# Output matmuls after a per-step plan with a queue, and a last block whose outputs keep tokens on partitions

## The chip, the core and the metric

The kernel runs on one core of a Trainium2 chip. The metric is the device time in microseconds (us), the median over several runs. Engines that matter: PE (TensorE matmuls), DVE (VectorE), ACT (ScalarE), POOL (GpSimd), and the queues that issue DMAs: SP's, ACT's and POOL's.

## The reference

Four batches of 12416 tokens with 128 channels. Per batch, 32 inducing vectors first attend over all tokens, then the tokens attend over the 32 results; a gated layer with 1536 hidden columns follows.

```python
def mab(q, kv):
    s = scale * (q @ kv.transpose(0, 2, 1))
    s = s - s.max(-1, keepdims=True)
    a = np.exp(s)
    a /= a.sum(-1, keepdims=True) + 1e-09
    return a @ kv
h = mab(I, x)
x = mab(x, h).astype(np.float32)
gate = 1.0 / (1.0 + np.exp(-(x @ w_gate)))
val = x @ w_val
out = (gate * val @ w_out).astype(np.float32)
```

The kernel never forms the second attention's output. It multiplies `h` into the weights first (`hw = h @ w_gate` and `h @ w_val`, 32 rows for each batch), so a token's gate and value columns are its 32 attention weights times `hw`. The sigmoid is computed as a tanh: with T = tanh(g/2), gate times value is 0.5 (T + 1) v.

## The kernel before

**Blocks and steps.** Tokens are taken in 97 blocks: 24 per batch of 512 tokens each, and one mixed last block of 4 times 128 tail tokens. The 1536 hidden columns are 12 chunks `j` of 128. The main loop (L709) does a block `n` in four steps `k`; step `k` handles the chunks 3k, 3k+1 (called va) and 3k+2 (vb). All engines follow the order of the program (`manual_schedule`, L70), each in its own queue.

In a step PE first fills the PSUM tile `va` (two matmuls, `v_fill`), then one pair of gate chunks `g` (`g_next`, `g_fill`), then some output matmuls, then `vb`, then in k1 and k3 a second `g` pair, or in k2 of some blocks a side job, and then more output matmuls. ACT turns each `g` pair into T (`g_tanh`, L421). DVE computes u = (T + 1) v, once for `va` and once for `vb` (`v_mul`, L434). The output matmuls (`out_mm`, L450) add `w_out` times u into one accumulator tile per block; after the twelfth, `out_store` (L455) scales it by 0.5 on ACT into `oT` (L460), transposes it by a DMA from SP (L462), and POOL stores it (L465, for the last block L472).

**Which output matmuls stand where.** They always belong to the u of the step before (`prev`, three of them). The first `first` of them go ahead of `vb`, the rest after it:

```python
first = 0 if k == 1 else 1
outs(prev[:first])
```

So a block's twelve outputs start in its k1 and end in k0 of the next block, after that step's `vb`.

**Tiles.** PSUM: `g` has two slots, shared with side jobs; `va`, `vb` and the accumulator `acc` have one each (L60 to L63). The gate pairs lead by three (`LEADP`). Most `g` and all `va` matmuls contract over 32 rows and take a quarter of the array each, so four of them run side by side; two of the six gate pairs (2 and 5) and all `vb` use weights padded with zeros to all 128 rows (`hwp`, `PADG`, `PADV`), the full array.

**Side jobs** (`put`, `extra`, `do_extra`, L650): work for the next batch and for later blocks, in k2 of 15 blocks of 24 for the first three batches and of three in the last, besides one in block 0 (batch-relative: s2 in 2, 10, 18; s1 in 4, 8, 11; s1t in 5; h in 7, 9, 12 to 15; hfin in 16; hw in 17). s1 and s2 end in an exp on ACT, h in an addition into `hacc` on DVE. Loads of x (`load_x`, POOL), transposes (`xT_dma`, SP) and the attention weights of later blocks are attached to steps by `at`.

**Start.** The six quarters of 2048 tokens of batch 0 are loaded by POOL, each with one DMA, then the weights. For each quarter, PE transposes 16 chunks (`xT_pe`; the first half is copied by ACT, the second by DVE), computes scores (`s1n`, with an exp on ACT) and adds them into h (`h_mm`).

Of the kernel before, what the change touches and what calls it, by code (L numbers as in the profile page):

```python
# [1 line left out]

# [6 lines left out]
F32 = mybir.dt.float32  # L9
F16 = mybir.dt.float16  # L10
AF = mybir.ActivationFunctionType
# [4 lines left out]
P = 128  # L16
TOK = 512
QT = 4 * TOK
M = 32
# [3 lines left out]
def kernel(  # L23
# [9 lines left out]
    nc = tc.nc  # L33
    B, N, C = x.shape
    m = inducing.shape[0]
    F = moe_w_gate.shape[1]
    NJ = F // P
    NP2 = NJ // 2
    SCALE = float(1.0 / (C ** 0.5))
    NQ = N // QT  # L40
    TAIL = N - NQ * QT
    NT0 = NQ * QT
# [5 lines left out]
    const = ctx.enter_context(tc.tile_pool(name="const", bufs=1))  # L48
    pers = ctx.enter_context(tc.tile_pool(name="pers", bufs=1))
    xtp = ctx.enter_context(tc.tile_pool(name="xtp", bufs=2))  # L50
    xqp = ctx.enter_context(tc.tile_pool(name="xqp", bufs=7))
    ep = ctx.enter_context(tc.tile_pool(name="ep", bufs=2))
    ap_ = ctx.enter_context(tc.tile_pool(name="ap", bufs=2))
    repp = ctx.enter_context(tc.tile_pool(name="repp", bufs=2))
    tp = ctx.enter_context(tc.tile_pool(name="tp", bufs=2))
    up = ctx.enter_context(tc.tile_pool(name="up", bufs=6))
    outp = ctx.enter_context(tc.tile_pool(name="outp", bufs=3))
    smp = ctx.enter_context(tc.tile_pool(name="smp", bufs=2))

# [5 lines left out]
    def slot_g(name):  # L65
        return ps_g.tile([P, 2 * TOK], F32, tag="g", name=name)
# [7 lines left out]
    def slot_o(name):  # L74
        return ps_o.tile([P, TOK], F32, tag="acc", name=name)
# [4 lines left out]
    xqs = {}  # L80

    def load_x(b, q):
        t = xqp.tile([P, QT], F16, tag="xq", name=f"xq_{b}_{q}")
        nc.gpsimd.dma_start(  # L84
            t[:], x[b, ds(q * QT, QT)].rearrange("(p j) c -> p (j c)", j=QT // P)
        )
        xqs[(b, q)] = t
# [4 lines left out]
    def load_tail(b):  # L92
# [12 lines left out]
    wo16 = const.tile([P, NJ, C], F16, tag="wo16")  # L105
    ident = const.tile([P, P], F16, tag="ident")
# [5 lines left out]
        out=ident[:], in_=ident[:], compare_op=ALU.not_equal, fill=1.0, base=0,  # L112
        pattern=[[-1, P]], channel_multiplier=1,
    )
    for q in range(2, NQ):
        load_x(0, q)
    nc.gpsimd.dma_start(wg16[:], moe_w_gate.rearrange("c (j f) -> c j f", f=P))
    nc.gpsimd.dma_start(wv16[:], moe_w_val.rearrange("c (j f) -> c j f", f=P))
    nc.gpsimd.dma_start(wo16[:], moe_w_out.rearrange("(j p) c -> p j c", p=P))
    nc.gpsimd.memset(stack[:], 0.0)  # L120
    for r in range(4):
        nc.gpsimd.affine_select(
            out=stack[:], in_=stack[:], compare_op=ALU.not_equal, fill=1.0,
# [3 lines left out]
    xTs = [xtp.tile([P, NT0], F16, tag="xT", name=f"xT_{b}") for b in range(B)]  # L127
# [23 lines left out]
    a1n = {}  # L151
# [23 lines left out]
    def s1n_mm(ps, b, q, lo, hi):  # L175
        for tk in range(lo, hi):
            j, r = tk % 4, tk // 4
            nc.tensor.matmul(
                ps[:, ds((j * 4 + r) * M, M)], xTs[b][:, ds(q * QT + tk * P, P)], indT[:],
                start=True, stop=True,  # L180
            )
# [10 lines left out]
    def h_mm(ps, b, q, first, last, tail, ch=0, cs=P):  # L192
        for j in range(4):
            nc.tensor.matmul(  # L194
                ps[:, cs:cs + P], ones[:, 0:P], a1n[(b, q)][:, j, :],
                start=first and j == 0, stop=last and j == 3,
            )
            if tail and j == 0:
                nc.tensor.matmul(
                    ps[:, cs:cs + M], ones[:, 0:P], a1n[(b, "t")][:], start=False, stop=False  # L200
                )
        for j in range(4):
            for r in range(4):
                nc.tensor.matmul(  # L204
                    ps[r * M:(r + 1) * M, ch:ch + P],
                    a1_chunk(b, q, 4 * r + j),
                    xqs[(b, q)][:, ts(4 * r + j, P)],
                    start=first and j == 0,
                    stop=last and j == 3 and not (tail and r == 0),
                )  # L210
        if tail:
            nc.tensor.matmul(
                ps[0:M, ch:ch + P], a1n[(b, "t")][:], xtail[:, b, :], start=False, stop=last,
            )
# [133 lines left out]
    NBK = len(blocks)  # L348
# [60 lines left out]
    Ts = {}  # L409
# [20 lines left out]

    def v_mul(ps, bi, j0, n):
        T = blocks[bi]["T"]
        u = up.tile([P, 2, TOK], F16, tag="u", name=f"u_{bi}_{j0}")
        nc.vector.scalar_tensor_tensor(  # L434
            out=u[:, 0:n, 0:T], in0=Ts[bi][:, j0:j0 + n, 0:T], scalar=1.0,
            in1=ps[:].rearrange("p (a t) -> p a t", t=TOK)[:, 0:n, 0:T],
            op0=ALU.add, op1=ALU.mult,
        )
        return [(bi, j0 + jj, u[:, jj, 0:T]) for jj in range(n)]

    accs = {}
    done_out = {}

    def out_mm(bi, j, u):
        T = blocks[bi]["T"]
        if bi not in accs:
            accs[bi] = slot_o(f"acc_{bi}")
            done_out[bi] = 0
        c = done_out[bi]
        nc.tensor.matmul(  # L450
            accs[bi][:, 0:T], wo16[:, j, :], u, start=(c == 0), stop=(c == NJ - 1)
        )
        done_out[bi] = c + 1

    def out_store(bi):  # L455
        k = blocks[bi]
        T = k["T"]
        nch = T // P
        oT = outp.tile([P, TOK], F16, tag="oT", name=f"oT_{bi}")
        nc.scalar.activation(out=oT[:, 0:T], in_=accs[bi][:, 0:T], func=AF.Copy, scale=0.5)  # L460
        on = outp.tile([P, 4, C], F16, tag="on", name=f"on_{bi}")
        nc.sync.dma_start(on[:, 0:nch, :], oT[:, 0:T], transpose=True)  # L462
        if not k["mixed"]:
            row0 = k["b"] * N + (2 * k["d"] + k["i"]) * QT
            nc.gpsimd.dma_start(  # L465
                out[ds(row0, QT)].rearrange("(p j) c -> p j c", j=QT // P)[
                    :, 4 * k["r"]:4 * k["r"] + 4, :],
                on[:],
            )
        else:  # L470
            for b in range(B):
                nc.gpsimd.dma_start(out[ds(b * N + NT0, P)], on[:, b, :])  # L472


    def xT_pe(b, q):
        for half in range(2):
            ps = slot_g(f"xt_{b}_{q}_{half}")
            v = ps[:].bitcast(F16)
            for j in range(8):
                nc.tensor.transpose(  # L480
                    v[:, ts(j, P)], xqs[(b, q)][:, ts(8 * half + j, P)], ident[:]
                )
            dst = xTs[b][:, ds(q * QT + half * 8 * P, 8 * P)]
            if half:
                nc.vector.tensor_copy(out=dst, in_=v[:, 0:8 * P])  # L485
            else:
                nc.scalar.copy(out=dst, in_=v[:, 0:8 * P])

    ps = slot_a("warm")
    warm(ps, 16)  # L490
# [3 lines left out]
    ps = slot_b("indT")  # L494
    v = ps[:].bitcast(F16)
# [4 lines left out]
    ps = slot_a("s1t_0")  # L500
# [1 line left out]
    s1t_exp(0, ps)  # L502

    hps = slot_a("h_0")
    def s1n(q):
        an = ep.tile([P, 4, P], F16, tag="a1q", bufs=3, name=f"a1q_0_{q}")
        ps = (slot_o if q % 2 else slot_b)(f"s1n_0_{q}")
        s1n_mm(ps, 0, q, 0, 16)
        nc.scalar.activation(
            out=an[:].rearrange("p j f -> p (j f)"), in_=ps[:, 0:TOK], func=AF.Exp, scale=SCALE,  # L510
        )
        a1n[(0, q)] = an

    for s in range(NQ):
        if s >= 1:
            s1n(s - 1)
        xT_pe(0, s)
        if s >= 2:
            h_mm(hps, 0, s - 2, s == 2, False, s == 2, TOK, 0)
    s1n(NQ - 1)  # L520
    h_mm(hps, 0, NQ - 2, False, False, False, TOK, 0)
    h_mm(hps, 0, NQ - 1, False, True, False, TOK, 0)
    psd = slot_g("warm2")
    warm(psd, 1)
# [2 lines left out]
    ps = slot_b("hfin_0")  # L527
# [4 lines left out]
    def q_srcs(b, q, lo, hi):  # L532
# [7 lines left out]
    ps = slot_g("s2n_01")  # L540
# [8 lines left out]
        out=a2f[:], in0=e2s["q00"][:, 0:4, :],  # L549
        in1=e2s[("q00", "rc")][:, 0, 0:4].unsqueeze(2).to_broadcast((P, 4, M)), op=ALU.mult,  # L550
    )
    ps = slot_b("a2T_0")
    v = ps[:].bitcast(F16)
# [21 lines left out]
    extra = {}  # L575
# [121 lines left out]
        g_tanh(bi, p, gp)  # L697
        gdone += 1

    def outs(us):  # L700
        for u in us:
            out_mm(*u)
            if done_out[u[0]] == NJ:
                out_store(u[0])

    g_next()
    g_next()
    prev = []
    for n in range(NBK):  # L709
        for k in range(4):  # L710
            for f in ev.get((n, k), ()):
                f()
            gwant = min(NG, gwant + 1)
            ps = slot_a(f"va_{n}_{k}")
            v_fill(ps, n, 3 * k, 2)
            if gdone < gwant:
                g_next()
            ua = v_mul(ps, n, 3 * k, 2)
            first = 0 if k == 1 else 1
            outs(prev[:first])  # L720
            ps = slot_b(f"vb_{n}_{k}")
            v_fill(ps, n, 3 * k + 2, 1)
            if k % 2:
                gwant = min(NG, gwant + 1)
            post = None
            if k == 2 and n in extra:
                post = do_extra(*extra[n])
            elif gdone < gwant:
                g_next()
            ub = v_mul(ps, n, 3 * k + 2, 1)  # L730
            if post:
                post()
            outs(prev[first:])
            prev = ua + ub
    outs(prev)

    order.__exit__(None, None, None)

# [29 lines left out]
```

## Time and profile before

| | us |
|---|---|
| median of 9 runs (lowest, highest) | 764.36 (762.41, 768.62) |
| the profiled execution's own time | 765.72 |
| its span, first to last instruction | 764.0 |
| DVE busy in the span | 709.5 (93%) |
| PE busy | 663.8 (87%) |
| ACT busy | 656.3 (86%) |
| last `v_mul` ends, from the span's start | 754.2 |

Busy time counts an instruction from its start to its end. Neighbours on one engine overlap a little, [...] so a busy share is no measure of how much more an engine could take. "Idle before, releaser" gives how long an engine stood still ahead of a group and what ended that. In the timeline a row is: start, duration, engine, line, operation, tile written and tiles read, count, and in brackets the idle time ahead of it. The granted clock of TensorE was 0.995 of full speed.

### The profile page before, as it was taken

Reading aid. Unit: us, or ns where it says so; the run is one execution under the profiler, and the core shown is the slowest. Engines: PE = TensorE matmul, PEld = TensorE weight load, DVE = VectorE, ACT = ScalarE, POOL = GpSimd, SP = SyncE. Lnnn points to the kernel's source line nnn. Section 1 sums busy time; section 2 is a strip of 40 time slices with the busy share of each in tenths; the row PEclk is TensorE's granted clock in tenths of the full one; section 3 lists DMA queues with packets and bytes.
Section 4 is the critical chain, followed back from the end, with each engine's and each line's share of the span. In section 5 each row is a group of like instructions: output and inputs, shape, how many; then the busy total and the mean of one; then the engine's idle time right before and its main releaser. Section 6 shows DMA issues by size and latency. Waiting matters only on the chain.

```text
span 764.0 us, 12231 instructions
## 1 busy us (share of the span) xinstructions
PE 663.8 (87%) x4525; PEld 247.2 (32%) x4525; DVE 709.5 (93%) x838; ACT 656.3 (86%) x725; POOL 214.7 (28%) x328
## 2 busy tenths in 40 slices
PE   7888899988889889989888899998888888888884
PEld 5423333333333323333333333332333333333332
DVE  2699999999999989999999999999999999999994
ACT  4789898888899879889889989889889888889883
POOL 5236114305313312502511601612420430330001
PEclk9999999999999999999999999999999999999998
DMA  9497993422567997523456899542342452252222
GB/s 180 74 142 138 204 183 81 107 50 69 118 95 137 151 169 150 111 61 71 87 94 134 122 201 170 111 77 56 70 103 49 76 111 56 69 117 50 56 48 56
DMA packets 182300, 80.25 MB, mean 105 GB/s; under 512 B 165952, under 2 KB 166624, under 8 KB 182240
## 3 DMA queue, kind: packets, MB, share of 16 engines
q1 hardware_dynamic: 162112, 40.18, 32.0%
q0 software_dynamic: 20128, 39.30, 24.0%
q8 instruction: 35, 0.57, 0.3%
q14 instruction: 25, 0.20, 0.1%
HBM read 27.80 MB, written 25.43 MB: 70 GB/s over the span
## 4 chain that ended last, share of the span: by engine, by line
PE 46%; DVE 31%; ACT 16%; DMA 3%; issue 2%; POOL 1%; SPq 0%; POOLq 0%; DVEq 0%; ACTq 0%
DVE u L434 29%; ACT T L421 16%; PE acc L450 15%; PE va L366 14%; PE g L366 7%; PE vb L366 5%; DMA xq<-in_x_dram 2%; DMA xT<-xq 1%; PE h L204 1%; PE s L273 1%; DVE hacc L220 1%; PE s L655 1%; PE h L194 1%; DMA on<-oT 0%; DVE rc L310 0%
## 5 line engine op out<-in xcount | busy, mean ns | idle before, releaser
L421 ACT ACTIVATE T<-g 128x1024 f16<-128x1024 f32 x582 | 573.7, 1024 | 76.7 <-PE g L366 62.6
L434 DVE SCALAR_TENSOR_TENSOR u<-T,va 128x1024 f16<-128x1024 f16 x388 | 473.3, 1220 | 24.0 <-ACT T L421 17.1
L450 PE MATMUL acc<-u,wo 128*128 128x512 f16 x1164 | 365.1, 382 | 0.4 <-DVE u L434 0.4
L434 DVE SCALAR_TENSOR_TENSOR u<-T,vb 128x512 f16<-128x512 f16 x388 | 263.9, 680 | 0.0
L366 PE MATMUL va<-rep,hw 32*128 32x512 f16 x768 | 149.5, 381 | 58.7 <-DVE u L434 57.0
L465 POOL DMA_DIRECT2D out_dram<-on x96 | 52.7, 549 | 492.7 <-DMA on<-oT 483.6
L450 PEld LDWEIGHTS <-wo 128*128 128x128 f16 x1164 | 108.5, 97 | 171.2 <-issue 88.5
L366 PE MATMUL vb<-rep,hwp 128*128 128x512 f16 x384 | 144.9, 377 | 19.0 <-DVE u L434 19.0
L366 PE MATMUL g<-rep,hw 32*128 32x512 f16 x768 | 148.8, 385 | 0.3 <-ACT T L421 0.2
L366 PEld LDWEIGHTS <-hw 32*128 32x128 f16 x1536 | 55.2, 91 | 219.3 <-issue 217.8
L366 PE MATMUL g<-rep,hwp 128*128 128x512 f16 x384 | 113.9, 378 | 2.9 <-DVE hT L239 1.8
L366 PEld LDWEIGHTS <-hwp 128*128 128x128 f16 x768 | 74.3, 97 | 78.8 <-issue 50.7
L320 POOL TENSOR_TENSOR a<-e2n,rc 128x512 f16<-128x512 f16 x88 | 89.2, 1041 | 8.1 <-DVE rc L310 7.8
L460 ACT ACTIVATE oT<-acc 128x512 f16<-128x512 f32 x97 | 58.6, 604 | 4.1 <-PE acc L450 4.1
L302 POOL TENSOR_TENSOR tree<-tree 128x256 f32<-128x256 f32 (+2 forms) x33 | 16.2, 490 | 2.6
L302 POOL TENSOR_TENSOR tree<-e2n 128x512 f32<-128x512 f16 x11 | 12.6, 1145 | 11.7 <-DMA e2n<-e 11.7
L84 POOL DMA_DIRECT2D xq<-in_x_dram x24 | 13.5, 567 | 0.8 <-POOLq L752 0.8
L485 DVE COPY xT<-xt 128x1024 f16<-128x1024 f16 x6 | 4.2, 692 | 9.8 <-PE xt L480 9.8
L163 ACT ACTIVATE e<-s 128x1024 f16<-128x1024 f32 x9 | 9.2, 1024 | 3.6 <-PE s L655 3.5
L280 ACT ACTIVATE e<-s 128x1024 f16<-128x1024 f32 x11 | 11.3, 1024 | 0.0
L139 PE MATMUL warm<-ones 128*128 128x512 f16 x23 | 7.9, 487 | 1.5 <-DVE ones L97 1.5
L259 POOL COPY hwp<-hw 32x128 f16<-32x128 f16 x16 | 4.6, 288 | 15.0 <-ACT hw L252 14.3
(89 smaller groups left out, 155.7 us busy)
## 6 DMA issues: line engine op xcount, KB each, us to landing
out_dram<-on POOLq DMA_DIRECT2D x96, 256.0 KB, 2.7
xq<-in_x_dram POOLq DMA_DIRECT2D x24, 512.0 KB, 6.9
on<-oT SPq DMA_TRANSPOSE x97, 2.4
wg<-in_moe_w_gate_dram POOLq DMA_DIRECT2D x1, 384.0 KB, 16.3
wv<-in_moe_w_val_dram POOLq DMA_DIRECT2D x1, 384.0 KB, 17.7
wo<-in_moe_w_out_dram POOLq DMA_DIRECT2D x1, 384.0 KB, 18.9
rep<-a SPq DMA_TRANSPOSE x22, 4.3
xT<-xq SPq DMA_TRANSPOSE x18, 5.3
```

The costliest lines, as they stand in the source:

```text
L84: nc.gpsimd.dma_start(t[:], x[b, ds(q * QT, QT)].rearrange("(p j) c -> p (j c)", j=QT // P))
L139: nc.tensor.matmul(ps[:, 0:TOK], ones[:, 0:P], ones[:], start=True, stop=True)
L163: nc.scalar.activation(out=e1[:, 0:w], in_=ps[:, 0:w], func=AF.Exp, scale=SCALE)
L280: nc.scalar.activation(out=e2[:], in_=ps[:], func=AF.Exp, scale=SCALE)
L302: nc.gpsimd.tensor_tensor(out=nxt, in0=cur[:, :, 0:w], in1=cur[:, :, w:2 * w], op=ALU.add)
L320: nc.gpsimd.tensor_tensor(out=a2[:, r], in0=e2n[:, i, :, r, :].unsqueeze(2).to_broadcast((P, 4, 4, M)), in1=rc[:, i, :, r].unsqueeze(2).un ...
L366: nc.tensor.matmul(ps[:, ds(col, TOK)], weights(k["b"]), rep[rows, 4 * k["i"] + k["r"]], start=True, stop=True,)
L421: nc.scalar.activation(out=Ts[bi][:, 2 * p:2 * p + 2, 0:T], in_=ps[:].rearrange("p (a t) -> p a t", a=2)[:, :, 0:T], func=AF.Tanh, scale=0.5,)
L434: nc.vector.scalar_tensor_tensor(out=u[:, 0:n, 0:T], in0=Ts[bi][:, j0:j0 + n, 0:T], scalar=1.0, in1=ps[:].rearrange("p (a t) -> p a t", t= ...
L450: nc.tensor.matmul(accs[bi][:, 0:T], wo16[:, j, :], u, start=(c == 0), stop=(c == NJ - 1))
L460: nc.scalar.activation(out=oT[:, 0:T], in_=accs[bi][:, 0:T], func=AF.Copy, scale=0.5)
L465: nc.gpsimd.dma_start(out[ds(row0, QT)].rearrange("(p j) c -> p j c", j=QT // P)[:, 4 * k["r"]:4 * k["r"] + 4, :], on[:],)
```

## The change

1. The output matmuls go through a queue `ready`. A plan says how many a step takes ahead of `vb` and after it, with another row for blocks that have a side job. A step may now take u of the step before and what was left over.
2. The tile u gets a tag for each width, with five buffers each, in place of six of the larger; `xq` goes from seven buffers to six.
3. The last block's outputs come with tokens on partitions: u is the stationary operand, `w_out` the moving one, four matmuls of 128 columns for each chunk. Two ACT copies with the factor 0.5 go to an f32 tile, and four DMAs on SP's and ACT's queues store it, with no transpose.
4. At the start, the last quarter of batch 0 is loaded in two halves, its scores and exps are made in two halves, and `h_mm` of earlier quarters is put between them.

```diff
-    xqp = ctx.enter_context(tc.tile_pool(name="xqp", bufs=7))
+    xqp = ctx.enter_context(tc.tile_pool(name="xqp", bufs=6))
...
-    up = ctx.enter_context(tc.tile_pool(name="up", bufs=6))
+    up = ctx.enter_context(tc.tile_pool(name="up", bufs=5))
...
-    for q in range(2, NQ):
+    for q in range(2, NQ - 1):
         load_x(0, q)
+    xl = xqp.tile([P, QT], F16, tag="xq", name=f"xq_0_{NQ - 1}")
+    xqs[(0, NQ - 1)] = xl
+    for half in range(2):
+        nc.gpsimd.dma_start(
+            xl[:, ts(half, QT // 2)],
+            x[0, ds((NQ - 1) * QT, QT)].rearrange("(p j) c -> p (j c)", j=QT // P)[
+                :, ts(half, QT // 2)],
+        )
...
-        u = up.tile([P, 2, TOK], F16, tag="u", name=f"u_{bi}_{j0}")
+        u = up.tile([P, n, TOK], F16, tag=f"u{n}", name=f"u_{bi}_{j0}")
...
     def out_mm(bi, j, u):
         T = blocks[bi]["T"]
+        if bi == NBK - 1:
...
+            c = done_out[bi]
+            for b in range(B):
+                nc.tensor.matmul(
+                    accs[bi][:, ts(b, P)], u[:, ts(b, P)], wo16[:, j, :],
+                    start=(c == 0 and b == 0), stop=(c == NJ - 1), skip_group_check=True,
+                )
+            done_out[bi] = c + 1
+            return
...
     def out_store(bi):
         k = blocks[bi]
+        if k["mixed"]:
+            o32 = outp.tile([P, B, C], F32, tag="o32", bufs=1, name="o32")
+            for h in range(0, B, 2):
+                w = min(2, B - h)
+                nc.scalar.activation(
+                    out=o32[:, h:h + w, :].rearrange("p b c -> p (b c)"),
+                    in_=accs[bi][:, ds(h * P, w * P)], func=AF.Copy, scale=0.5,
+                )
+                for b in range(h, h + w):
+                    eng = nc.sync if b % 2 == 0 else nc.scalar
+                    eng.dma_start(out[ds(b * N + NT0, P)], o32[:, b, :])
+            return
...
-    def xT_pe(b, q):
+    def xT_pe(b, q, half):
...
-    def s1n(q):
+    def s1n(q, halves=((0, 16),)):
...
+        for lo, hi in halves:
+            ps = (slot_o if (q + (lo > 0)) % 2 else slot_b)(f"s1n_0_{q}_{lo}")
+            s1n_mm(ps, 0, q, lo, hi)
+            r0, r1 = lo // 4, hi // 4
+            nc.scalar.activation(
+                out=an[:].rearrange("p j (r m) -> p j r m", m=M)[:, :, r0:r1, :],
+                in_=ps[:, 0:TOK].rearrange("p (j r m) -> p j r m", j=4, m=M)[:, :, r0:r1, :],
+                func=AF.Exp, scale=SCALE,
+            )
     for s in range(NQ):
         if s >= 1:
             s1n(s - 1)
-        xT_pe(0, s)
-        if s >= 2:
+        xT_pe(0, s, 0)
+        if s == NQ - 1:
             h_mm(hps, 0, s - 2, s == 2, False, s == 2, TOK, 0)
-    s1n(NQ - 1)
+        xT_pe(0, s, 1)
+        if 2 <= s < NQ - 1:
+            h_mm(hps, 0, s - 2, s == 2, False, s == 2, TOK, 0)
+    s1n(NQ - 1, ((0, 8),))
     h_mm(hps, 0, NQ - 2, False, False, False, TOK, 0)
+    s1n(NQ - 1, ((8, 16),))
     h_mm(hps, 0, NQ - 1, False, True, False, TOK, 0)
...
-    def outs(us):
-        for u in us:
+    ready = deque()
+
+    def outs(count):
+        for _ in range(min(count, len(ready))):
+            u = ready.popleft()
             out_mm(*u)
             if done_out[u[0]] == NJ:
                 out_store(u[0])
+    PLAN = ((2, 3), (1, 1), (2, 2), (1, 2))
+    PLAN_JOB = ((2, 3), (1, 1), (1, 1), (1, 2))
...
+            c0, c1 = (PLAN_JOB if n in extra else PLAN)[k]
...
-            first = 0 if k == 1 else 1
-            outs(prev[:first])
+            ready.extend(prev)
+            outs(c0)
...
-            outs(prev[first:])
+            outs(c1)
             prev = ua + ub
-    outs(prev)
+    ready.extend(prev)
+    outs(len(ready))
```

More of the change, by code (lines that the diff above doesn't have):

```diff
@@ L1 @@
+from collections import deque
 from contextlib import ExitStack
@@ L432, in v_mul @@
         T = blocks[bi]["T"]
-        u = up.tile([P, 2, TOK], F16, tag="u", name=f"u_{bi}_{j0}")
+        u = up.tile([P, n, TOK], F16, tag=f"u{n}", name=f"u_{bi}_{j0}")
         nc.vector.scalar_tensor_tensor(
-            out=u[:, 0:n, 0:T], in0=Ts[bi][:, j0:j0 + n, 0:T], scalar=1.0,
+            out=u[:, :, 0:T], in0=Ts[bi][:, j0:j0 + n, 0:T], scalar=1.0,
             in1=ps[:].rearrange("p (a t) -> p a t", t=TOK)[:, 0:n, 0:T],
@@ L445, in out_mm @@
         T = blocks[bi]["T"]
+        if bi == NBK - 1:
+            if bi not in accs:
+                accs[bi] = slot_o(f"acc_{bi}")
+                done_out[bi] = 0
+            c = done_out[bi]
[6 more added lines that the diff above has]
+            return
         if bi not in accs:
@@ L456, in out_store @@
         k = blocks[bi]
-        T = k["T"]
-        nch = T // P
+        if k["mixed"]:
[10 more added lines that the diff above has]
+            return
@@ L459, in out_store @@
         oT = outp.tile([P, TOK], F16, tag="oT", name=f"oT_{bi}")
-        nc.scalar.activation(out=oT[:, 0:T], in_=accs[bi][:, 0:T], func=AF.Copy, scale=0.5)
+        nc.scalar.activation(out=oT[:], in_=accs[bi][:], func=AF.Copy, scale=0.5)
         on = outp.tile([P, 4, C], F16, tag="on", name=f"on_{bi}")
[L462 to L468, printed above, removed]
-            )
-        else:
-            for b in range(B):
-                nc.gpsimd.dma_start(out[ds(b * N + NT0, P)], on[:, b, :])
@@ L475, in xT_pe @@
-    def xT_pe(b, q):
[L476 to L487, printed above, removed]
+        nc.sync.dma_start(on[:], oT[:], transpose=True)
@@ new lines, in out_store @@
+        row0 = k["b"] * N + (2 * k["d"] + k["i"]) * QT
+        nc.gpsimd.dma_start(
+            out[ds(row0, QT)].rearrange("(p j) c -> p j c", j=QT // P)[
+                :, 4 * k["r"]:4 * k["r"] + 4, :],
+            on[:],
+        )
+    def xT_pe(b, q, half):
+        ps = slot_g(f"xt_{b}_{q}_{half}")
+        v = ps[:].bitcast(F16)
+        for j in range(8):
+            nc.tensor.transpose(
+                v[:, ts(j, P)], xqs[(b, q)][:, ts(8 * half + j, P)], ident[:]
+            )
+        dst = xTs[b][:, ds(q * QT + half * 8 * P, 8 * P)]
+        if half:
+            nc.vector.tensor_copy(out=dst, in_=v[:, 0:8 * P])
+        else:
+            nc.scalar.copy(out=dst, in_=v[:, 0:8 * P])
@@ L504 @@
     hps = slot_a("h_0")
-    def s1n(q):
[L506 to L512, printed above, removed]
+    def s1n(q, halves=((0, 16),)):
+        if (0, q) not in a1n:
+            a1n[(0, q)] = ep.tile([P, 4, P], F16, tag="a1q", bufs=3, name=f"a1q_0_{q}")
+        an = a1n[(0, q)]
+        for lo, hi in halves:
[6 more added lines that the diff above has]
+                func=AF.Exp, scale=SCALE,
+            )
     for s in range(NQ):
```

## The prediction

> **What bounds the kernel now.** I read the page first: shares of busy time, then the costliest groups.
>
> ```profile
> span 764.0 us, 12231 instructions
> ...
> PE 663.8 (87%) x4525; PEld 247.2 (32%) x4525; DVE 709.5 (93%) x838; ACT 656.3 (86%) x725; POOL 214.7 (28%) x328
> ...
> L434 DVE SCALAR_TENSOR_TENSOR u<-T,va 128x1024 f16<-128x1024 f16 x388 | 473.3, 1220 | 24.0 <-ACT T L421 17.1
> ...
> L434 DVE SCALAR_TENSOR_TENSOR u<-T,vb 128x512 f16<-128x512 f16 x388 | 263.9, 680 | 0.0
> L366 PE MATMUL va<-rep,hw 32*128 32x512 f16 x768 | 149.5, 381 | 58.7 <-DVE u L434 57.0
> ```
>
> VectorE is nearest to full: 388 steps (97 blocks of four, k0 to k3) each hold a va multiply of 1220 ns and a vb multiply of 680 ns. The va row of PE says that PE waits for VectorE in only part of the steps. So I took the starts of successive va multiplies from VectorE's timeline: the medians from k0 to k1, k1 to k2, k2 to k3, k3 to k0 are 1.76, 1.99, 1.84 and 1.765 us. The loss sits in k1 (nearly every block) and k2 (blocks with a side job). One block, k0 at 195.87 to k3 at 201.38, in the timeline of all engines:
>
> ```profile
> 195.87 1.22 DVE L434 SCALAR_TENSOR_TENSOR u<-T,va 128x1024 f16<-128x1024 f16 x1
> ...
> 196.88 0.60 ACT L460 ACTIVATE oT<-acc 128x512 f16<-128x512 f32 x1
> ...
> 197.15 0.39 PE L366 MATMUL va<-rep,hw 32*128 32x512 f16 x2 [0.37 <-DVE u L434]
> ...
> 197.63 1.22 DVE L434 SCALAR_TENSOR_TENSOR u<-T,va 128x1024 f16<-128x1024 f16 x1
> 197.74 0.38 PE L366 MATMUL vb<-rep,hwp 128*128 128x512 f16 x1 [0.20 <-DVE u L434]
> ...
> 198.39 0.81 PE L450 MATMUL acc<-u,wo 128*128 128x512 f16 x3
> ...
> 199.13 0.39 PE L366 MATMUL va<-rep,hw 32*128 32x512 f16 x2
> ...
> 199.46 0.39 PE L450 MATMUL acc<-u,wo 128*128 128x512 f16 x1
> ...
> 199.62 1.22 DVE L434 SCALAR_TENSOR_TENSOR u<-T,va 128x1024 f16<-128x1024 f16 x1 [0.17 <-ACT T L421]
> ```
>
> See first the on-time step: the next va pair may go 1.28 after a va multiply began (195.87 to 197.15; slot a is single), the multiply follows 0.48 later: floor 1.76. In k1 the three trailing output matmuls hold the va pair until 199.13, 1.50 after 197.63: late by 0.22, and the step takes 1.99. The "ACT T" at 199.62 is not the cause: that tanh (pair 3) was done at 198.64.
>
> Constants from the same rows: a full-array matmul goes 0.32 after a 32-row group begins (199.13 to 199.46), full ones follow each other by 0.215 ((0.81-0.38)/2), a 32-row pair goes 0.31 after the last full one begins (198.82 to 199.13). oT begins 0.44 after the last output matmul of a block begins, or 0.90 after the tanh ahead of it; its accumulator bank is free 0.66 after its start (0.60 and 0.06).
>
> [...] here 16 transposes with their weight loads take 1.05 us, 0.055 each, so four 128-column outputs cost what one of 512 does. [...] SP's two plain DMAs here took 0.40 and 0.41.
>
> **The plan.** k0 to k3 issued 1+2, 0+3, 1+2, 1+2 outputs (before vb + after). With the queue they issue 2+1, 1+1, 2+2, 1+2; in a block with a job k2 issues 1+1, and the next k0 2+3. Times from the step's va multiply, PE's own group ahead at -0.48, so the first output at -0.16:
>
> - k0 (2+1): vb 0.27, output 0.485, free for va at 0.795. After a job (2+3): last output 0.915, free 1.225. Both under 1.28: 1.76.
> - k1 (1+1): its first output is now the next block's first, and there is one accumulator bank: it waits for oT. Normally oT starts at k0+1.02, bank free at k0+1.68 = k1-0.08: vb 0.135, full g pair 0.35 and 0.565, output 0.78, free 1.09. Step 1.76: 0.225 gained. After a job the fifth output of k0 starts at 0.915, so oT at k0+1.355, bank free at k1+0.255: vb 0.47, g 0.685 and 0.90, output 1.115, free 1.425. Late 0.145: step 1.905, only 0.085 gained. Queued behind the waiting output on PE are vb and the g pair; the vb multiply (needed at 1.14, there at 0.47+0.48) is covered, the tanh of that g pair starts at 1.32 instead of 0.985.
> - k2 without a job (2+2): free 1.01; unchanged 1.76.
> - k2 with an s job (s1, s2; 1.95 now): one output less behind it, free at 1.28 instead of 1.47. But the exp then frees its g slot 0.085 too late for k3, so k2 and k3 gain 0.105 together. If the block before had a job too, the tanh at 1.32 delays the slot that the job needs; with k3's wait the pair of steps loses 0.06. Jobs h, hfin, hw: 2.07, 2.70, 1.84, set by hacc (0.416) and the rec chain on VectorE or the job's own start: nothing.
> - k3 (1+2) unchanged, no slack (free at 1.28).
>
> ScalarE has room: back-to-back tanhs start 0.92 apart (195.06, 195.98), 6x0.92+0.52 = 6.0 per block against a floor of 7.05. VectorE's other work is untouched.
>
> Sum. Per batch of 24 blocks for the first three: 15 blocks follow a job (x0.085 = 1.28), 9 do not (x0.225 = 2.03), s jobs alone 2x0.105, s jobs after jobs 4x-0.06: 3.27, times 3 = 9.8. Last batch: 3x0.085 + 21x0.225 + 2x0.105 = 5.2. Loop: **15.0**.
>
> **Last block.** Rows of the end:
>
> ```profile
> 753.53 0.68 DVE L434 SCALAR_TENSOR_TENSOR u<-T,vb 128x512 f16<-128x512 f16 x1
> 753.67 0.97 PE L450 MATMUL acc<-u,wo 128*128 128x512 f16 x3 [0.37 <-DVE u L434]
> 754.68 0.60 ACT L460 ACTIVATE oT<-acc 128x512 f16<-128x512 f32 x1 [4.10 <-PE acc L450]
> 755.30 1.19 SPq L462 DMA_TRANSPOSE on<-oT  x1
> 758.23 2.10 POOL L472 DMA_DIRECT2D out_dram<-on  x4 [6.33 <-DMA on<-oT]
> ```
>
> From the last multiply's end (754.21) to the span's end (763.95) is 9.75: output and latency 0.47, oT 0.60, transpose to 757.7, four POOL issues to 760.33, landing about 761.8, some 2.0 of closing. After: outputs 0.6 (weights are now u, loaded after the multiply), copy of 256 columns 0.39 (between 278 ns for 128 and 497 for 384 columns at L387), DMA issue on ScalarE's own queue ahead of the second copy 0.4 to 0.8 (alone, or behind SP's), second copy 0.39, landing 1.8 (SP's 64 KB load of xt took 1.8), closing 2.0: 5.6 to 6.0. Gain 3.75 to 4.15, I take **4.0**. SP's queue is empty by then (its last transpose before was issued near 748.4), and POOL's stores of the block before went at 751.37. If an f32 store of 64 KB to DRAM from SP or ScalarE (no row of before) cost 2 us more, 2; if the two queues' issues overlap wholly, 4.5.
>
> **Start-up.** Now s1n of quarter 5 begins at 21.75 (its ScalarE copy waits for exp of quarter 4), exp 22.41 to 23.01, last h at 23.06. After, ScalarE's copy stays at 20.69 to 21.70; first half s1n 21.75, exp 22.2 to 22.6; h of quarter 4 to 22.65; VectorE's copy of half two, its transposes now behind h of quarter 3 (0.65), ends 22.55; second s1n 22.65, exp 23.1 to 23.5, last h 23.55: **0.4 lost** (two exps, 0.39 each, for one of 0.60). Splitting the load gains nothing here: quarter 5 lands at 19.6 (issued 4.6, landing 15.0) and is first used at 19.95; were it later, the halves could win up to 1. One more POOL issue (0.55) lies ahead of wg, wv, wo; wv lands at 23.4, is used at 25.35: hidden. On POOL the constants behind it are needed only at 24.2 and 26.85. xqp 6: quarter 0 of the next batch takes a buffer free since 13.8, no wait. u in two tags: five each, more than the at most five outputs waiting, no wait.
>
> **Total.** 15.0 + 4.0 - 0.4 = 18.6: span 764.0 to 745.4. The profiled run had 765.72 by its own clock, 1.7 around the span; the median of the nine is 764.36. So 764.36 - 18.6 = **745.8**.
>
> **Rivals.** (A) The bank never binds after jobs, nor the g slots: 97x0.225 + 18x0.19 = 25.2, tail 4.0, start-up 0: **735.2**. For: the margin is 0.145, a fifth output issued a little earlier would halve it. Against: PE issues in order, and oT can't start before the twelfth output. (B) The change doesn't do what it says: k1's lateness is the tanh named in the row at 199.62, so k1 keeps 1.99 and only the ends move: 764.36 - 3.6 = **760.8**. Against: that tanh ended 0.98 earlier. (C) Slower: the first output of k1 waits in every block for an oT that starts late. The step equals 1.99 when the bank frees at k1+0.34; with the tail's 3.6 spread over 97 blocks it decides at k1+0.38, oT at k0+1.48 instead of 1.02. With oT behind one more half tanh, k0+1.75, the step is 2.30: +30 - 3.6, **791**. Against: oT stands behind pair 3's tanh only, and ScalarE idles 0.69 in each k3. The xT waits of side jobs (0.9 us at block 8, 2.6 at block 32) can move a us or two either way.
>
> **How the numbers follow.** Forecast (741 to 751) 0.55, A (733 to 741) 0.25, B or half of it (751 to 761) 0.13, C 0.05, no change 0.02. The range 735 to 755 leaves out some of A, half of B, and C. Within 0.3% (2.3 us) is about what this measurement can't tell from no change.
>
> **What would show it.** k1 at 1.76 in blocks after a block without a job, 1.90 after a job, with PE's first output of k1 waiting for oT (L460) there; PE's wait for VectorE growing by some 20 us; k2 of s jobs near 1.76 with k3 longer; from last multiply to end under 6.2. Wrong if k1 is 1.76 everywhere (A), or vb or g come so late that VectorE waits.

## The result, and the profile after

The changed kernel takes 751.38 us (median of 10 runs, 747.02 to 753.87) against 764.36, 13.0 less. The ratio of the means is 0.9815 with a 95% interval of 0.9791 to 0.9839, which is 14.2 us. The forecast was 745.8 in a range of 735 to 755: faster, as said, but 18.6 us were worked out. The profiled execution took 751.15 with a span of 749.4; before it was 765.72 and 764.0, so the two traces differ by 14.6. All ratios below are of means too, against runs of the kernel before on the same chip, whose medians were 764.06 to 765.88. (One line number in the text ahead of the prediction is off: the order by hand is set at L77.)

The page of the changed kernel, the lines that answer to those shown of before:

```profile
span 749.4 us, 12313 instructions
...
PE 673.4 (90%) x4561; PEld 256.2 (34%) x4561; DVE 709.1 (95%) x838; ACT 647.1 (86%) x727; POOL 213.1 (28%) x325
...
L443 DVE SCALAR_TENSOR_TENSOR u<-T,va 128x1024 f16<-128x1024 f16 x388 | 473.2, 1220 | 13.0 <-issue 4.9
L472 PE MATMUL acc<-u,wo 128*128 128x512 f16 x1152 | 378.0, 383 | 15.0 <-ACT oT L492 15.0
```

VectorE does the same work (709.1 against 709.5 us busy) in a shorter span. New is PE's wait of 15.0 us ahead of the output matmuls, ended by oT on ScalarE: the one accumulator bank.

The starts of the va multiplies, again from VectorE's timeline, cut the trace into three parts:

| us | before | after | gain | forecast |
|---|---|---|---|---|
| span's start to the first va multiply | 29.22 | 30.75 | -1.53 | -0.4 |
| first to last va multiply | 723.17 | 711.76 | 11.41 | 15.0 |
| of these: k2 and k3 of the nine blocks with an s1 job | 37.03 | 40.65 | -3.62 | about 0 |
| of these: all other steps | 686.14 | 671.11 | 15.03 | 15.0 |
| last va multiply to the span's end | 11.56 | 6.89 | 4.67 | 4.0 |

The steps by kind (medians of the distance from one va multiply to the next) stand close to the forecast: k1 after a block without a job 1.76 (forecast 1.76), after a job 1.88 (1.905); k2 and k3 of an s2 job alone 1.78 and 1.84, together 3.62 (3.605), of an s2 job after a job 1.83 and 1.93, together 3.76 (3.77). Block 8 of the first batch shows both that and what went otherwise. Its timeline, all engines, from k0's outputs to the end of k2; the block before it had a job:

```profile
91.33 0.81 PE L472 MATMUL acc<-u,wo 128*128 128x512 f16 x3
...
92.17 0.60 ACT L492 ACTIVATE oT<-acc 128x512 f16<-128x512 f32 x1 [0.34 <-PE acc L472]
...
92.60 1.22 DVE L443 SCALAR_TENSOR_TENSOR u<-T,va 128x1024 f16<-128x1024 f16 x1
...
92.82 0.38 PE L472 MATMUL acc<-u,wo 128*128 128x512 f16 x1 [0.32 <-ACT oT L492]
93.04 0.38 PE L375 MATMUL vb<-rep,hwp 128*128 128x512 f16 x1
...
93.25 0.59 PE L375 MATMUL g<-rep,hwp 128*128 128x512 f16 x2
93.69 0.38 PE L472 MATMUL acc<-u,wo 128*128 128x512 f16 x1
...
94.48 1.22 DVE L443 SCALAR_TENSOR_TENSOR u<-T,va 128x1024 f16<-128x1024 f16 x1
...
94.96 0.40 PE L691 MATMUL s<-xT,indT 128*32 128x512 f16 x4
...
96.01 0.40 PE L691 MATMUL s<-xT,indT 128*32 128x512 f16 x4 [0.65 <-DMA xT<-xq]
...
97.15 1.22 DVE L443 SCALAR_TENSOR_TENSOR u<-T,va 128x1024 f16<-128x1024 f16 x1 [0.85 <-issue]
```

k0 of this block began at 90.84. Its third output after vb was the fifth of the step, so oT began at 92.17, 1.33 after k0 (forecast 1.355), and PE's first output of k1 had to wait until 92.82. The next va multiply came 1.88 after 92.60. Then the s1 job: its second half stood still until a transpose of x landed, and k2 took 2.67. Who waits for whom on PE, longest first, after and then before:

```profile
PE va L375 <- DVE u L443: 31.5, 107, 0.8
PE acc L472 <- ACT oT L492: 15.0, 48, 0.4
PE s L691 <- DMA xT<-xq: 5.4, 5, 1.5
```

```profile
PE va L366 <- DVE u L434: 57.0, 152, 1.2
PE vb L366 <- DVE u L434: 19.0, 95, 0.2
PE s L655 <- DMA xT<-xq: 3.2, 2, 2.4
```

Columns: us in total, times, longest. PE's wait for VectorE in va did not grow, as I had said it would, but fell from 57.0 to 31.5, and its wait ahead of vb (19.0) is no longer among those shown. The work of PE is the same and the steps are shorter, so its idle time shrinks (from 100 us of the span to 76).

The end of the changed kernel, all engines:

```profile
743.65 0.68 DVE L443 SCALAR_TENSOR_TENSOR u<-T,vb 128x512 f16<-128x512 f16 x1
743.79 1.00 PE L462 MATMUL acc<-wo,u 128*128 128x128 f16 x12 [0.35 <-DVE u L443]
744.82 0.38 ACT L483 ACTIVATE o<-acc 128x256 f32<-128x256 f32 x1 [3.88 <-PE acc L462]
745.23 1.18 SPq L489 DMA_DIRECT2D out_dram<-o  x2
745.24 0.38 ACTq L489 DMA_DIRECT2D out_dram<-o  x1
745.67 0.39 ACT L483 ACTIVATE o<-acc 128x256 f32<-128x256 f32 x1 [0.46 <-ACT o L483]
746.08 0.37 ACTq L489 DMA_DIRECT2D out_dram<-o  x1
```

From the last multiply's end (744.33) to the span's end it is 5.1 us, forecast 5.6 to 6.0, before 9.75. The issue on ScalarE's own queue holds the second copy for 0.46, near the lower of my two values. The higher one, 0.8 behind SP's issue, was an estimate from SP's 0.40 and 0.41; here SP's first issue and ScalarE's began at 745.23 and 745.24, and the four took 0.34 to 0.38 each.

### The profile page after: what moved, and what is told of

Read it like the earlier page. It is cut to its first block, busy times and chain, and to the rows that moved or that the text cites. A ratio compares the mean times of both kernels' runs of the same rounds, so it can differ in the third digit from the quotient of the medians.

```text
span 749.4 us, 12313 instructions
## 1 busy us (share of the span) xinstructions
PE 673.4 (90%) x4561; PEld 256.2 (34%) x4561; DVE 709.1 (95%) x838; ACT 647.1 (86%) x727; POOL 213.1 (28%) x325
## 3 DMA queue, kind: packets, MB, share of 16 engines
q1 hardware_dynamic: 161856, 40.18, 31.5%
## 4 chain that ended last, share of the span: by engine, by line
PE 42%; DVE 40%; ACT 6%; DMA 6%; issue 4%; SPq 1%; POOL 1%; DVEq 0%; ACTq 0%; POOLq 0%
DVE u L443 39%; PE acc L472 16%; PE va L375 12%; PE g L375 6%; PE vb L375 4%; DMA xT<-xq 4%; ACT oT L492 4%; ACT T L430 2%; DMA xq<-in_x_dram 2%; PE s L282 1%; PE s L691 1%; PE h L213 1%; PE h L203 1%; SPq L494 0%; PE xt L507 0%
## 5 line engine op out<-in xcount | busy, mean ns | idle before, releaser
L430 ACT ACTIVATE T<-g 128x1024 f16<-128x1024 f32 x582 | 566.6, 1024 | 61.7 <-PE g L375 54.5
L472 PE MATMUL acc<-u,wo 128*128 128x512 f16 x1152 | 378.0, 383 | 15.0 <-ACT oT L492 15.0
L375 PE MATMUL va<-rep,hw 32*128 32x512 f16 x768 | 149.8, 381 | 39.9 <-DVE u L443 31.5
L472 PEld LDWEIGHTS <-wo 128*128 128x128 f16 x1152 | 100.3, 97 | 166.5 <-issue 96.8
L375 PEld LDWEIGHTS <-hw 32*128 32x128 f16 x1536 | 58.0, 91 | 191.8 <-issue 183.5
L311 POOL TENSOR_TENSOR tree<-e2n 128x512 f32<-128x512 f16 x11 | 12.6, 1145 | 11.7 <-DMA e2n<-e 11.7
L691 PE MATMUL s<-xT,indT 128*32 128x512 f16 x72 | 6.5, 385 | 5.6 <-DMA xT<-xq 5.4
L203 PEld LDWEIGHTS <-ones 128*128 128x128 f16 x96 | 7.4, 101 | 7.5 <-issue 5.7
```

Source lines behind the costliest of these rows:

```text
L203: nc.tensor.matmul(ps[:, cs:cs + P], ones[:, 0:P], a1n[(b, q)][:, j, :], start=first and j == 0, stop=last and j == 3,)
L311: nc.gpsimd.tensor_tensor(out=nxt, in0=cur[:, :, 0:w], in1=cur[:, :, w:2 * w], op=ALU.add)
L375: nc.tensor.matmul(ps[:, ds(col, TOK)], weights(k["b"]), rep[rows, 4 * k["i"] + k["r"]], start=True, stop=True,)
L430: nc.scalar.activation(out=Ts[bi][:, 2 * p:2 * p + 2, 0:T], in_=ps[:].rearrange("p (a t) -> p a t", a=2)[:, :, 0:T], func=AF.Tanh, scale=0.5,)
L472: nc.tensor.matmul(accs[bi][:, 0:T], wo16[:, j, :], u, start=(c == 0), stop=(c == NJ - 1))
L691: nc.tensor.matmul(ps[r * M:(r + 1) * M, ts(i, TOK)], indT[:], xTs[a[0]][:, ds(q * QT + r * TOK, TOK)], start=True, stop=True,)
```

## The experiments

The theory: the steps went as worked out; the difference to the forecast is the s1 jobs' wait for the transposes of x, which do not get faster with the loop (from issue to landing 5.3 us before and 5.5 after, medians of 18), and the start. The rivals: the plan itself gives less than the parts say, or the bank is not what makes k1 1.88.

**The plan alone, the last block alone, the old start.** Three kernels. The first is the kernel before with the queue, the plan and the u tags:

```diff
+    PLAN = ((2, 3), (1, 1), (2, 2), (1, 2))
+    PLAN_JOB = ((2, 3), (1, 1), (1, 1), (1, 2))
...
-            outs(prev[:first])
+            ready.extend(prev)
+            outs(c0)
```

> The kernel before with the queue and the plan alone (and the u tags, xq at six); start-up and last block as before. Theory (the parts add: loop 11 to 15 us, last block 4 to 5, start-up a loss of 0.4 to 1.5): k1 at 1.76 after a block without a job and 1.88 after a job, first va multiply at 29.2 us as before, 764.4 - 11 to -15, so 749 to 753. Rival (the parts help each other, or the gain is mostly in the ends): 757 or more with the plan alone.

Measured: 754.23 us, ratio 0.9866 (0.9823 to 0.9908), k1 at 1.76 and 1.88, first va multiply at 28.94. The median lies a little above the 749 to 753 expected, but the kernel before had 765.88 on this chip, and the 11.7 less are within the 11 to 15. All steps but those of the s1 jobs take 671.6 us, against 686.1 before; k2 and k3 of the s1 blocks take 40.0.

The second is the kernel before with the new `out_mm` and `out_store` for the last block:

```diff
+        if k["mixed"]:
+            o32 = outp.tile([P, B, C], F32, tag="o32", bufs=1, name="o32")
```

> The kernel before with the new last block alone. Theory: from the start of the last va multiply to the end of the span 6.9 us instead of 11.6, the rest unchanged: 764.4 - 4.7 = 759.7. Rival (the end is set by something else than the transpose and POOL's stores, such as the closing): under 2 us of gain, above 762.4.

Measured: 760.31, ratio 0.9939 (0.9914 to 0.9964); from the last va multiply to the end 6.8 us. The tail's gain stands by itself. In this trace the s1 blocks took 34.1 us in k2 and k3, so with the old loop the wait for xT is sometimes nearly absent.

The third is the changed kernel with the old start:

```diff
-        xT_pe(0, s, 0)
-        if s == NQ - 1:
-            h_mm(hps, 0, s - 2, s == 2, False, s == 2, TOK, 0)
-        xT_pe(0, s, 1)
+        xT_pe(0, s)
```

> The changed kernel with the load, the transposes and the score order of the start as before. Theory (the start-up edit costs 0.4 by its order and about 1 by a PE clock at half speed after a longer wait for the load of quarter 4): first va multiply at 29.2 to 29.7 instead of 30.75, 750 +- 1. Rival (the load waited longer by chance and the split load gains): first va multiply at 30.7 or later, no gain.

Measured: 750.80, ratio 0.9809 (0.9757 to 0.986); first va multiply at 29.01, 1.7 earlier than in the changed kernel. But the whole is no faster than the changed kernel by what the runs can tell: k1 of block 0 took 3.31 instead of 2.18, PE's wait for xT was 9.0 us in this trace instead of 5.4, and the s1 blocks took 44.2 instead of 40.7. What the start gave, block 0 and the s1 jobs gave back.

**The bank.** The changed kernel with

```diff
             c0, c1 = (PLAN_JOB if n in extra else PLAN)[k]
+            if k == 1 and n - 1 in extra:
+                c0, c1 = 0, 2
```

> The changed kernel; in a block after a block with a job, k1 issues no output ahead of vb and two after it, so that no matmul of the step stands behind the wait for oT. Theory (PE waits for the one accumulator bank): k1 after a job 1.76 to 1.78 instead of 1.88, PE's wait for oT (15 us in 48 waits) gone, s jobs after jobs 1.78 and 1.84 instead of 1.83 and 1.93; 49 x 0.12 + 6 x 0.14 = 6.7 us less: 744.7. Rival (in those steps PE is late by its five outputs in k0 or by VectorE's own work): k1 stays at 1.88, 751.

Measured: k1 after a job 1.77, s2 after a job 1.76 and 1.84, and the wait for oT is gone. Steps other than the s1 ones fell to 665.2 us, 5.9 less than in the changed kernel (6.7 expected, s1 included), though k1 of block 0 took 1.35 more here. So it is the bank that made the 1.88. Yet the time was 750.20, ratio 0.9813 (0.9761 to 0.9865): not the 744.7 expected. The waits of this kernel and the s1 job of block 32 say where it went:

```profile
PE vb L375 <- DVE u L443: 9.8, 49, 0.2
PE s L691 <- DMA xT<-xq: 9.7, 5, 4.2
```

```profile
267.96 0.40 PE L691 MATMUL s<-xT,indT 128*32 128x512 f16 x4
...
272.55 0.40 PE L691 MATMUL s<-xT,indT 128*32 128x512 f16 x4 [4.20 <-DMA xT<-xq]
...
273.93 1.22 DVE L443 SCALAR_TENSOR_TENSOR u<-T,va 128x1024 f16<-128x1024 f16 x1 [4.56 <-issue]
```

PE stood for 4.2 us in the middle of an s1 job, and VectorE 4.56 behind it. The wait for xT is now 9.7 us in all, 4.3 more than in the changed kernel, and the s1 blocks take 45.8, 5.2 more. vb waits for VectorE in 49 blocks by 0.2 each, with no effect: that is PE being early.

**More time for the transposes.** If s1 only comes too early, it may be put later. In the changed kernel, the jobs' plan by block, with s1t moved from block 5 to 4 and its tail loaded with the first quarter:

```diff
-                ((1, 0), (2, 0), (2, 2), (3, 2), 4, (5, 2), (7, 9)),
-                ((5, 0), (6, 0), (6, 2), (7, 2), 8, (9, 2), (12, 13)),
+                ((1, 0), (2, 0), (2, 2), (3, 2), 5, (5, 3), (7, 8)),
+                ((5, 0), (6, 0), (6, 2), (7, 2), 9, (10, 2), (12, 13)),
```

> The changed kernel with the first two s1 jobs of a batch one block later (4 to 5, 8 to 9; s1t to 4 with its tail loaded and transposed first, the second h to 8), so that the transposes of x have a block more. Theory (what the loop gave back is the wait of s1 for xT): the wait of PE's s matmuls for xT falls from 5.4 to under 1.5 us and no s1 step is above 2.1, time 751.4 - 4 to -6: 746. Rival (SP's queue is full, so that the delay only moves to the next transpose, such as a1n before h): PE waits some 5 us elsewhere for a DMA, 751.

Measured: 749.68, ratio 0.9773 (0.9724 to 0.9823). Mixed: s1's wait for xT fell to 1.2 us, but k2 of block 4, where s1t now stands, took 5.89 us, and s1 in block 11 of the third batch 3.25. s1t itself did not wait: its matmul went at 65.47, 0.33 after the step's va multiply. What held the step is VectorE's reciprocal for the s2 job of block 2:

```profile
70.76 0.35 DVE L319 RECIPROCAL rc<-rs 128x32 f32<-128x32 f32 x1 [3.80 <-POOL rs L311]
71.03 1.16 DVE L443 SCALAR_TENSOR_TENSOR u<-T,va 128x1024 f16<-128x1024 f16 x1
```

It needs sums that GpSimd makes from e2n, another tile that SP's queue transposes. GpSimd stood 4.71 us for the transpose of an output (on) and 0.64 for e2n, and began the sums at 67.56. With this edit the tail's transpose goes into that queue ahead of e2n (60.84 and 63.38; in the changed kernel e2n went at 58.79, the tail at 62.92). The rival is partly right: the delay moved to the next work that reads a late transpose. The start was at 30.60 again.

With the bank's edit as well:

> The same, and k1 after a job with no output ahead of vb and two after it. Theory: both gains at once, since the transposes no longer hold the loop: bank waits gone (6.7) and xT waits gone (4 to 6): 740 to 742, k1 at 1.77. Rival (as above, the loop is bound to the transposes): 749 to 751.

Measured: 742.50, ratio 0.970 (0.966 to 0.9741); k1 1.77, s1's wait for xT 2.8 us, k2 of block 4 still 3.84, again with VectorE behind those sums (1.75 us). Both gains now show together, half a us above the 740 to 742 of the theory.

The control is the kernel before with the same moved jobs:

> The kernel before with the s1 jobs later in the same way. Theory: its s1 steps waited 3.2 us for xT in the profiled execution, mostly at one place, so at most 3 to 4 us are there: 761 to 763. Rival (later jobs help by something else than the wait, for instance by the order of the jobs): a gain as large as in the changed kernel, 759 or less.

Measured: 763.80, ratio 0.9979 (0.9961 to 0.9996), with no wait for xT among the waits shown. Later jobs are worth 2 us or so in the old loop. In the changed loop they are worth 3 us or so (ratio 0.9773 after 0.9815, with intervals that overlap), and with the bank's edit more than 8 (0.970 after 0.9813).

**The rest of the waits, and the start.** s1t goes to block 6, which had no job, with its tail as in the kernel before, and the last transpose of a batch half a block earlier; the later s1 jobs and the bank's edit stay:

```diff
-                ((8, 0), (9, 0), (9, 3), (10, 2), 11, (12, 2), (14, 15)),
+                ((8, 0), (9, 0), (9, 3), (10, 0), 11, (12, 2), (14, 15)),
...
-            put(n0 + 5, "s1t", nb)
+            put(n0 + 6, "s1t", nb)
```

> The changed kernel with k1 after a job at none ahead and two after vb, the first two s1 jobs a block later, s1t in block 6 (free before) and the last xT transpose of a batch half a block earlier. Theory (what is left in e6 is the wait of s1t in block 4 and of s1 in block 11 for their transposes, some 5 us): steps above their kind's usual length under 3 us in sum, 738 to 740. Rival (SP's queue of transposes holds the loop wherever the jobs stand): 742 or more, with a wait in a new place.

Measured: 738.97, ratio 0.9653 (0.9616 to 0.9689). Steps over 0.3 us above the median of their kind still summed to 5.3 us, more than expected: 2.9 and 0.8 of it in k2 and k3 of block 7, where h waited for the transpose of the scores (a1n), and no s1 job waited for an xT. The expectation had the wait of block 4 wrong, as above; with the tail's transpose behind e2n again the reciprocal there waits 0.20 us and the step takes 2.29. How much each of the moves gave was not separated. First va multiply at 29.74.

The same with the old start:

> The same with the start of the kernel before. Theory (the start-up edit loses by its order 0.4, and when quarter 4 lands late another us by the half clock): first va multiply at 28.9 to 29.2, 0.5 to 1.5 us faster than e8. Rival (the start-up edit is neutral, as in e4): within 0.3 of e8.

Measured: 736.89, ratio 0.9639 (0.9595 to 0.9682): the best kernel of this study, 27.2 us under the kernel before on its own chip (764.06) and some 14 under the changed one. Its waits on PE, longest first, hold no side job's DMA any more; the last line is the load of quarter 4 at the start:

```profile
PE va L367 <- DVE u L435: 33.4, 107, 0.8
PE vb L367 <- DVE u L435: 9.8, 49, 0.2
...
PE xt L500 <- DMA xq<-in_x_dram: 1.1, 1, 1.1
```

The medians of the last two kernels differ by 2.1 us and the traces by 4.3: 0.8 is the start (28.96 against 29.74) and 3.6 are block 7, since the wait for a1n did not come in this trace. So the start alone is not settled by these two times. It is also the only trace in which TensorE's granted clock stays at 1.00 in every 2 us from 4 us on (its mean is 0.999; the others have 0.991 to 0.998).

**The start and the clock.** Two kernels, each run once, take the start's edit apart: first the split load with the old order.

> The changed kernel with quarter 5 loaded in two halves, but the order of transposes and scores as before. Theory: the split alone costs nothing at the start, first va multiply 28.9 to 29.2. Rival (one more load ahead of the weights delays the start): 29.5 or later.

Measured: first va multiply at 29.03, so the split costs the start nothing. (The run took 755.93, with 10.6 us of waits for xT in s1.) Then one load with the new order.

> The changed kernel with quarter 5 loaded in one piece, but the new order of transposes and scores. Theory: the order costs, first va multiply 29.4 to 30.8, later when PE waits over an us for quarter 4. Rival: 28.9 to 29.2.

Measured: 29.54. The run took 751.04. Over all traces the old order gave 28.92 to 29.22 in seven kernels; the new one 28.95, 29.54, 29.74, 29.77, 30.60 and 30.75 in six. These starts hold more than the order: the scores of quarter 4, which stand ahead of the part whose order differs, begin anywhere from 18.87 to 20.15. From the beginning of these scores to the first va multiply the new order takes 10.08 or 10.09 us in four traces, the old one 9.68 to 9.79 in the four where PE did not wait for quarter 5 (up to 9.96 in the others). So the order costs 0.3 to 0.4. The two high values, the changed kernel's among them (10.60 and 10.85 by this count), are those where PE's clock fell ahead of the first va multiply. The changed kernel's windows (stretch, its length, busy time of PE, its weight loads, VectorE, ScalarE and GpSimd with counts, granted clock, DMA share, GB/s):

```profile
16.00:18.00 2.00, 0.33 (x14) 0.23 (x11) 0.00 (x0) 0.60 (x1) 0.00 (x0) 1.00 1.05 177
18.00:20.00 2.00, 2.00 (x36) 1.75 (x36) 0.69 (x1) 1.01 (x1) 0.00 (x0) 0.67 1.10 213
20.00:22.00 2.00, 2.00 (x42) 1.66 (x36) 0.00 (x0) 0.95 (x2) 0.00 (x0) 0.50 1.07 207
22.00:24.00 2.00, 1.97 (x61) 1.59 (x61) 0.69 (x1) 1.04 (x2) 0.00 (x0) 0.97 1.67 182
```

PE idled 1.67 us for the load of quarter 4, and for the next 4 us the granted clock is 0.67 and 0.50, just where the start is bound to PE.

The same fall comes later in other traces. In block 0, at 31 to 35 us, the clock goes down to about 0.50 in seven of the thirteen, with the old order (the changed kernel with the old start: k1 of block 0 3.31 us) and the new (with no output ahead of vb: 3.53). k1 of block 0 takes 3.3 to 3.9 us there, and 2.2 in the five kernels with the plan where it does not fall. It also comes after waits in the loop. In the changed kernel PE waits 1.54 us for xT in block 32, until 273.27; two windows follow:

```profile
274.00:276.00 2.00, 2.00 (x9) 0.63 (x10) 1.59 (x2) 1.82 (x3) 0.00 (x0) 0.67 0.73 117
276.00:278.00 2.00, 2.00 (x9) 0.43 (x8) 0.93 (x2) 1.58 (x2) 0.49 (x1) 0.50 0.67 129
```

and k3 of that block takes 2.89 us instead of 1.93. The length of the wait alone does not decide it: the kernel before waited 2.43 us for xT in its block 32, and the clock stayed at 1.00 (windows from 264 to 282 us). What sets the moment is not shown.

## Why the prediction was right, and where it was short

- **What bounds the kernel** held: VectorE's two multiplies with the floor of 1.76, and the trailing outputs of k1 that held va back. With them moved, k1 is 1.76.
- **The plan's steps** held within 0.03 us, the bank included; all steps but those of the s1 jobs gained 15.03 us, the sum said 15.0. That the sum fits so closely is partly luck: k1 after a job gained 4.8 us where about 4.1 were put, and steps that were put at nothing lost about as much. The experiment without outputs ahead of vb shows that the bank is the cause.
- **The last block**: right mechanism, 4.67 instead of 4.0 (the twelve output matmuls took 1.00 us where the three wide ones had taken 0.97, so four of 128 columns do cost what one of 512 does; the last store lands 1.8 us after its issue at 746.08, as assumed, and 1.5 of closing follow where 2.0 were put; the issue between the copies was near the lower bound).
- **The xT waits** are the term that was mis-sized. I wrote that they "can move a us or two either way" and left them out of the sum. They went one way: from 3.2 to 5.4 us in the profiled pair, where the s1 steps grew from 37.0 to 40.7 us (nine pairs of steps at the usual 1.95 and 1.76 would be 33.4). Of these 3.6 us, 2.2 are the wait and about 1.0 is k3 of block 32 at the lower clock after its wait, which the working did not have. With the plan and the s1 jobs in their old places the wait was 5.4 to 10.6 us in the six kernels tried. The 0.9 and 2.6 us in the trace of before were the sign: a job that already waits in two of nine places has no slack, and what is taken out of the blocks ahead of it can come back there. With the jobs moved, the gain of the bank's edit came out. That the faster loop lengthens this wait rests on these moves and on one trace for each kernel; the kernel with the new last block alone, whose loop is the old one, had 0.5. Which part of the transposes' way is slow (SP's queue in order, the transfers themselves, or the loads ahead) was not separated.
- **The start**: 1.53 lost instead of 0.4. The order's price, 0.3 to 0.4 in the traces at full clock, was right. The rest was not in the working: in the profiled pair the scores of quarter 4 began 0.6 later (PE waited 1.67 for its load instead of 1.20, and the 16 transposes then took 1.27 instead of 1.07 at the lower clock), and the lower clock took another 0.5 after that (10.60 against 10.08). The clock fell ahead of the first va multiply in two of six traces of the new order and in none of seven of the old; whether the order brings it about is not shown, since in block 0, with k1 at 3.3 us and more, it fell with both.
- In medians: 18.6 forecast, 13.0 measured. In the traces, 14.6: 15.0 - 3.6 + 4.7 - 1.5.
- Rival A (735.2) needed the bank not to bind after jobs; it did bind. Taking it away with the jobs moved and the old start came to 736.9. That this is so near is in part chance: the s jobs gain about 0.1 us each and not the 0.19 of the rival, and the moved jobs also took away waits that the kernel before had. B and C did not come.

## What to carry to other kernels

When a loop gets faster, look at every wait in it that does not scale with it, above all those that are already on the edge: a side job that waits a little in some places has no slack left. Price each at the time that is taken out ahead of it, and move the job in the same change. See too what PE's clock does after a wait: here, at 0.50, that could cost another us (k3 of block 32 2.89 us instead of 1.93). In an in-order queue, put nothing that may wait for a shared bank ahead of work that others need soon: two outputs after vb instead of one on each side cost nothing and freed 0.11 us in each block after a job.

## What the runs showed of the hardware

- A wait of PE of 1.46 and 1.67 us at the start was followed by 4 us at a granted clock of 0.50 to 0.73; after waits of 0.9 to 1.2 us there, in other runs, it stayed at 1.00 for the next 6 us and more.
- In the main loop PE waited 15 times for a DMA for 1.5 us or more, over all traces. With eight of these waits (1.54 to 4.20 us) the granted clock fell to 0.50, with seven (1.53 to 2.43 us) it did not. k3 behind the eight took 2.38 to 3.21 us. Where the windows of a whole fall stand here, it took about the same: in the changed kernel's block 32 they show 0.67, 0.50 and 0.97, which is 2 x (0.33 + 0.50 + 0.03) = 1.72 us of clock, as much as 3.4 us at 0.50; its start gives 1.72 too, and the start of the kernel with the later s1 jobs (0.73, 0.50, 0.92) 1.70.
- Two stores of 64 KB from SP and two from ScalarE landed 1.6 and 1.8 us after issue (medians); ScalarE's next copy began 0.46 us after the one before it had ended, with an issue of 0.38 between them.
- Two va and two g matmuls over 32 rows began within 0.01 us of each other and each pair took 0.39 us (92.11 and 92.12 in the changed kernel); the two g matmuls over 128 rows at 93.25 took 0.59.
- VectorE's neighbours overlap: of the kernel before, the va multiply at 195.87 took 1.22 and the vb multiply began at 197.01, 0.08 before its end.
- Steps of one kind mostly repeat within 0.02 us (124 of the 136 steps in the changed kernel's blocks without a job in them or in the block before); what varies between the traces sits in the few steps that wait for a DMA, in k1 of block 0, and in the steps after a fall of the clock.
